# Recurrent attention and a gated feed-forward on one core: diagonal sums of five groups by wide TensorE products, and a new order of loads and steps

## The chip, the cores and the metric

One Trainium2 chip, one of its cores. The metric is the device time of one execution in microseconds. The core has five engines that run their own queues of instructions in order: TensorE (PE in the rows, its weight loads PEld), VectorE (DVE), ScalarE (ACT), GpSimd (POOL) and SyncE (SP, which here only issues DMAs). They wait for one another by semaphores.

## The reference

Four sequences of 768 steps with 8 heads of 48: a state of 48 x 48 per head decays by w, takes the outer product of k and v, and is read by r; the current step is weighted by u. The result goes through a feed-forward with a convolution over three steps and a sigmoid gate.

```
for t in range(S):
    kt, vt, rt = (k[:, :, t], v[:, :, t], r[:, :, t])
    cur = np.einsum('bhd,bhe->bhde', u[None] * kt, vt)
    y[:, :, t] = np.einsum('bhd,bhde->bhe', rt, state + cur)
    state = w[None, :, :, None] * state + np.einsum('bhd,bhe->bhde', kt, vt)
# x = y as (B, S, 384)
h = np.maximum(x @ w_in, 0.0)
conv_out = sum(conv_w[k] * hp[:, k:k + S, :] for k in range(3))   # hp: h padded
gate = 1.0 / (1.0 + np.exp(-conv_out))
return h * gate @ w_out
```

## The kernel before

**Attention.** The 4 x 768 steps are cut into 24 groups of 128 steps (GT), each of two chunks of 64 (C). Heads lie in pairs, one on partitions 0 to 47, the other on 64 to 111, so that two products run on separate halves of the array. A group has k and r feature-major (tile KR; its halves are called KK and RR), k, r and v token-major (TOK, three slots) and a score tile SC; four buffers each of KR and TOK turn round (NBUF), two of SC. `prep(g)` scales KR by powers of the decay, makes the scaled token-major k, and writes the diagonal of SC: for each step and head the sum over features of u k r, on the diagonal by a multiplication with `eye`. `visit(g, av, su)` is the work of PE: for group g the outputs AV (from state and from scores), and for group g+1 the scores SP and the state sums UP. After it VectorE copies SP into SC under a mask (line 659) and forms the two new states SS, each M + UP, where M is the old state times the decay. Visit -1 does group 0's scores only; visit 2 is split in two halves.

**How the diagonal sum is made before.** Groups 0 and 1 (NE = 2): VectorE multiplies KK by RR into SC, sixteen TensorE products of one column each (line 573) sum over features against `uw`, and VectorE multiplies by `eye` from PSUM (line 582). From group 2 on: GpSimd multiplies token-major r by k (KRT) and by u (KRU), VectorE sums (line 592), GpSimd multiplies by `eye`. Token-major k is made from KR by PE for group 0 alone (NK = 1, line 565, with a copy by ScalarE, line 576); later groups load it and GpSimd multiplies it by the tile TH (KS). TH itself comes from PE (line 491) and a ScalarE copy.

**Feed-forward.** Seven units of columns, each in eight slices. `first` is the product with w_in (line 741, into the banks HP0 and HP1), then ScalarE's relu and scale (749, 750), two convolution steps on VectorE (753), the sigmoid (756), the gate (757). `second` is the product with w_out (788 for the first unit, in full precision; 791 for the others, in three rounded products, for which the result is split in a high and a low part). The weights are loaded as w_in and w_out pieces of 384 KB into three staging buffers ST, converted on ScalarE and VectorE (504, 507, 509: the tile WF) and split into two rounded parts (ScalarE line 515; GpSimd the low part). The first unit reads the attention's output from XF; rows of head 6 and 7 are moved there by small DMAs from SBUF to SBUF, by SP and ScalarE.

**Order.** All steps are written down as a plan (`op`) with their reads and writes. `Plan.late` gives each step a due time, `MOVES` shifts due times, and `Plan.order` picks for each engine the next step; the engines then run these lists in order. Where PE would be without work before the first `second`, filler products of a zero tile `wz` (line 874) are put. Group loads and weight loads (classes in LONG) are limited: one may be issued only when the sixth before it has landed (LOADS = 6), from the fortieth on the fourth before it. Line 382 issues all DMAs, line 373 all `tensor_tensor` steps.

Of the kernel before, what the change touches and what calls it, by code (L numbers as in the profile page):

```python
# [16 lines left out]
C = 64  # L17
# [22 lines left out]
LONG, LOADS = ('ldK', 'ldT', 'ldV', 'wdma'), 6  # L40
NE = 2
NK = 1
# [19 lines left out]
FBASE, FETCH, FIRST, LATER = 3.4, 0.7, 40, 4  # L62
GATED = 4
DIRECT, ACTQ = (2,), (1,)
# [28 lines left out]
class Plan:  # L93
# [36 lines left out]
    def late(self):  # L130
# [16 lines left out]
        for seed, share, sigma, near in self.moves:  # L147
            x = seed
            for i in range(n):
                x = (x * 1103515245 + 12345) & 0x7fffffff  # L150
                u = x / 2147483648.0
                x = (x * 1103515245 + 12345) & 0x7fffffff
                if u < share and (not near or abs(late[i] - near) < 15.0):
                    late[i] += sigma * (2.0 * (x / 2147483648.0) - 1.0)
        return late

    def order(self):
# [25 lines left out]
        def fetched(s, t, k):  # L183
# [5 lines left out]
            while count > len(there) - 0.4:  # L189
                at_ = max(s, s + (len(there) - 0.4 - a) * d, there[-1])  # L190
                there.append(at_ + FBASE + FETCH * sum(1 for z in large[-8:] if z > at_))
# [5 lines left out]
        while todo:  # L197
            best = None
            for e in self.ENG:
# [13 lines left out]
                if e in ("sp", "act"):  # L213
                    y = large[-LOADS] if LOADS <= len(large) < FIRST else large[-LATER] if len(large) >= FIRST else 0.0
                    for i in av:
                        if self.dma[i]:
                            ready[i] = max(ready[i], lanes[0], y if ops[i][4] in LONG else 0.0)
# [52 lines left out]
            elif self.dma[i]:  # L270
# [5 lines left out]
                if cls in LONG:  # L276
                    large.append(done)
# [25 lines left out]
def rwkv_ffn_kernel(tc, krd, krt, vt, wd, ut, w_in, conv_w, w_out, out):  # L303
# [4 lines left out]
    with ExitStack() as ctx:  # L308
# [71 lines left out]
        def dma(rd, wr, dst, src, dur=0.5, x=0.1, cls="", q="sp", gate=None):  # L380
            def issue(e):
# [3 lines left out]
                if cls in LONG:  # L385
                    k = LOADS if len(loads) < FIRST else LATER
                    if len(loads) >= k:
                        tc.add_manual_dep(i.ins, loads[-k].ins.name, behind_, reason="loads")
                    loads.append(i)
# [146 lines left out]
        def bank(g):  # L536
            return [(HP[0], ("HP", 0)), (HP[1], ("HP", 1)), (PO[1], ("PO", 1))][g] if g < 3 else (UP, "UPq")

        def prep(g):
# [14 lines left out]
            if g < NE:  # L554
                kb, key = bank(g)
                pp = s[0:112].rearrange("q p c t -> q p (c t)")
                tt("dve" if g < 3 else ANY, 512, kr(i), [("SC", g % 2)], "P", out=pp, in0=KK[i][0:112], in1=RR[i][0:112], op=ALU.mult)

                def mm(e):
                    for c in range(2):  # L560
                        for p in range(NP):
                            for x in range(2):
                                r = slice(64 * x, 64 * x + D)
                                n = (p * 2 + c) * D
                                PE.matmul(kb[64 * x:64 * x + C, n:n + D], KK[i][r, p, c * C:(c + 1) * C], D64[r, p], start=True, stop=True)

                def mq(e):
                    for c in range(2):
                        for p in range(NP):
                            for x in range(2):  # L570
                                r = slice(64 * x, 64 * x + D)
                                n = NP * 2 * D + p * 2 + c
                                PE.matmul(kb[64 * x:64 * x + C, n:n + 1], s[r, p, c], uw[r, p:p + 1], start=True, stop=True)
                if g < NK:
                    op("pe", 1.1, [k for k in kr(i) if k[0] == "KK"] + ["D64"], [key], mm, "pks", 1700, mode=1, k=32)
                    op("act", act(384), [key], [("tK", i)], lambda e: A.copy(k_t.rearrange("q p c d -> q (p c d)"), kb[:, 0:NP * 2 * D]), "KSc")
                else:
                    tt(ANY, 384, ["TH"], [("tK", i)], "KS", out=k_t, in0=k_t, in1=TH.unsqueeze(2).broadcast_to([128, NP, 2, D]), op=ALU.mult)
                op("pe", 1.1, [("SC", g % 2), "uw"], [key], mq, "pq", 1200, mode=1, k=32)
                q = kb[:, NP * 2 * D:NP * 2 * D + H]  # L580
                if g < 3:
                    op("dve", dve(512, psum=1), [key, "eye"], [("SC", g % 2)], lambda e: V.tensor_tensor(
                        out=s.rearrange("q p c t -> q (p c) t"), in0=eye.unsqueeze(1).broadcast_to([128, 2 * NP, C]), in1=q.unsqueeze(2).broadcast_to([128, 2 * NP, C]), op=ALU.mult), "dg")
                    return
                op("act", 0.2, [key], [("QQ", g % 2)], lambda e: A.copy(QQ[g % 2], q), "qc")
                diagonal(g)
# [351 lines left out]
```

## Time and profile before

| what | value |
|---|---|
| median of 3 timed runs | 301.81 us (300.54 to 302.5) |
| profiled execution: span, first to last instruction | 302.5 us |
| PE busy | 287.7 us, 95% of the span |
| VectorE, ScalarE, GpSimd busy | 222.5, 176.4, 166.2 us |
| bytes moved by DMA | 37.00 MB, mean 122 GB/s |

The page's first part has each engine's busy time. The windows view gives it for stretches between two times, with the clock that PE was granted (1.00 is full speed). In the timeline a row is one or several instructions in a row of one kind: start, duration, engine, line, what is written and read, count, and in brackets the idle time ahead with what ended it. TensorE works an f32 product in two recorded passes, so that a product of the order counts as two records in the trace.

### The profile page before, as it was taken

To read this page: it belongs to the slowest core of one execution; us is meant where nothing else is said; L and a number is where in the kernel's file an instruction comes from. 1 tells how busy PE (TensorE), PEld (TensorE's weight loads), DVE (VectorE), ACT (ScalarE), POOL (GpSimd) and SP (SyncE) were. 2 spreads that over 40 slices of the span, in tenths; PEclk is the share of its full clock that TensorE was granted. 3 is DMA by queue.
4 is the path that set the end of the run, shared out by engine and by line. 5 is a ranking of instruction groups with operands and counts; after the bars stand their busy time and mean duration, and the time that the engine had idled before them with its cause. 6 is when DMAs were issued, how large, how long until landed. Compare 5 with 4: busy or idle time off the path is not lost.

```text
span 302.5 us, 9831 instructions
## 1 busy us (share of the span) xinstructions
PE 287.7 (95%) x4104; PEld 239.2 (79%) x4110; DVE 222.5 (74%) x359; ACT 176.4 (58%) x348; POOL 166.2 (55%) x196
## 2 busy tenths in 40 slices
PE   7979999869998999999999999999999999999994
PEld 2657666546777888889888888888888988899993
DVE  5766579896998876877879984899867755556561
ACT  3135484857776456664656753667735665556663
POOL 8367686984678884787735846658511111131230
PEclk9997999998999999999999999999999999999999
DMA  6994695855655535646424453554210020001102
GB/s 155 226 240 130 201 278 158 243 166 158 187 176 154 148 106 146 178 119 172 141 75 126 114 179 64 133 139 143 75 49 14 15 96 7 9 0 62 33 0 78
DMA packets 24011, 37.00 MB, mean 122 GB/s; under 512 B 6256, under 2 KB 16784, under 8 KB 23968
## 3 DMA queue, kind: packets, MB, share of 16 engines
q1 hardware_dynamic: 23632, 36.04, 42.7%
q8 instruction: 32, 0.52, 0.7%
q10 hardware_dynamic: 336, 0.35, 0.5%
q14 instruction: 11, 0.09, 0.1%
HBM read 29.49 MB, written 4.72 MB: 113 GB/s over the span
## 4 chain that ended last, share of the span: by engine, by line
PE 67%; DMA 6%; DVE 5%; POOL 4%; issue 3%; SPq 2%; ACT 2%; POOLq 0%; DVEq 0%; ACTq 0%
PE HP L741 29%; PE PO L791 25%; PE SP L638 4%; POOL TOK L373 3%; PE AV L654 3%; PE PO L788 3%; DMA TOK<-in_krt_dram 2%; PE AV L647 2%; SPq L382 2%; PE UP L651 2%; DMA KR<-in_krd_dram 1%; DMA ST<-in_w_in_dram 1%; DVE CV L753 1%; DVE KR L373 1%; DMA XF<-XF 1%
## 5 line engine op out<-in xcount | busy, mean ns | idle before, releaser
L741 PE MATMUL HP<-XT,wi 128*128 128x464 f32 (+2 forms) x432 | 98.8, 373 | 0.2 <-DVE CV L757 0.2
L791 PE MATMUL PO<-GG,wo 128*128 128x462 f32 (+2 forms) x432 | 97.5, 369 | 0.7 <-POOL GG L763 0.7
L753 DVE SCALAR_TENSOR_TENSOR CV<-HP,cw,CV 128x462 f32<-128x462 f32 (+2 forms) x112 | 75.2, 672 | 21.2 <-ACT CV L750 19.9
L791 PEld LDWEIGHTS PO<-GG,wo 128*128 128x128 f32 x432 | 80.2, 189 | 9.7 <-POOL GG L763 0.9
L741 PEld LDWEIGHTS HP<-XT,wi 128*128 128x128 f32 x432 | 79.5, 189 | 9.6 <-issue 0.4
L763 POOL TENSOR_TENSOR GG<-CV,GG 128x462 fp32r<-128x462 f32 (+2 forms) x30 | 34.7, 1156 | 65.6 <-ACT GG L762 61.0
L749 ACT ACTIVATE HP<-HP 128x464 f32<-128x464 f32 (+2 forms) x56 | 29.3, 523 | 50.4 <-PE HP L741 50.3
L638 PE MATMUL SP<-KR 48*64 48x64 f32 x768 | 46.3, 233 | 5.6 <-DVE KR L373 4.1
L757 DVE TENSOR_TENSOR CV<-HP,CV 128x462 f32<-128x462 f32 (+2 forms) x56 | 34.3, 612 | 21.3 <-ACT CV L756 21.0
L638 PEld LDWEIGHTS SP<-KR 48*64 48x64 f32 x768 | 38.9, 137 | 12.2 <-DVE KR L373 5.9
L654 PE MATMUL AV<-SC,TOK 64*48 64x64 f32 x760 | 47.0, 223 | 0.0
L647 PE MATMUL AV<-KR,SS 48*48 48x64 f32 x696 | 43.8, 223 | 0.0
L756 ACT ACTIVATE CV<-CV 128x462 f32<-128x462 f32 (+2 forms) x56 | 31.9, 569 | 19.8 <-DVE CV L753 19.6
L651 PE MATMUL UP<-TOK 64*48 64x48 f32 x704 | 41.3, 209 | 2.2 <-DVE SS L373 2.2
L750 ACT ACTIVATE CV<-HP,cw 128x462 f32<-128x462 f32 (+2 forms) x56 | 35.1, 627 | 2.3 <-ACT HP L749 0.4
L651 PEld LDWEIGHTS UP<-TOK 64*48 64x48 f32 x704 | 34.1, 127 | 2.3 <-DVE SS L373 2.3
L654 PEld LDWEIGHTS AV<-SC,TOK 64*48 64x48 f32 x760 | 35.7, 124 | 0.0
L647 PEld LDWEIGHTS AV<-KR,SS 48*48 48x48 f32 x696 | 32.5, 123 | 2.0 <-issue 2.0
L373 POOL TENSOR_TENSOR SC<-eye,QQ 128x512 f32<-128x512 f32 x22 | 23.4, 1064 | 18.0 <-PE AV L654 14.2
L762 ACT CAST GG<-CV 128x462 fp32r<-128x462 f32 (+2 forms) x48 | 27.2, 566 | 9.5 <-DVE CV L757 9.1
L373 POOL TENSOR_TENSOR TOK<-TOK 128x384 f32<-128x384 f32 x22 | 22.6, 1027 | 17.9 <-DMA TOK<-in_krt_dram 17.9
L373 POOL TENSOR_TENSOR MM<-SS,w 112x192 f32<-112x192 f32 x36 | 19.0, 528 | 17.1 <-DVE SS L373 15.7
(85 smaller groups left out, 358.8 us busy)
## 6 DMA issues: line engine op xcount, KB each, us to landing
KR<-in_krd_dram SPq DMA_DIRECT2D x46, 192.0 KB, 4.1
TOK<-in_krt_dram SPq DMA_DIRECT2D x22, 384.0 KB, 4.4
TOK<-in_vt_dram SPq DMA_DIRECT2D x47, 96.0 KB, 3.5
ST<-in_w_in_dram SPq DMA_DIRECT2D x8, 384.0 KB, 3.8
ST<-in_w_out_dram SPq DMA_DIRECT2D x8, 384.0 KB, 3.8
XT<-XT SPq DMA_DIRECT2D x126, 16.0 KB, 2.0
out_dram<-OS SPq DMA_DIRECT2D x6, 193.0 KB, 2.0
out_dram<-OS SPq DMA_DIRECT2D x5, 191.0 KB, 2.2
```

Of the source, the lines that this page charges most:

```text
L373: op(eng, d, rd, wr, lambda e: e.tensor_tensor(**kw), cls, port=not psum)
L638: PE.matmul(SP_[xs[x], p, c], KK[j][rows[x], p, t], RR[j][rows[x], p, t], start=True, stop=True)
L647: PE.matmul(outs[x], state(2 * g + c)[rows[x], p], RR[i][rows[x], p, t], start=not direct, stop=False)
L651: PE.matmul(UP[rows[x], n:n + D], TOK[j][xs[x], 0, p, c], TOK[j][xs[x], 2, p, c], start=True, stop=True)
L654: PE.matmul(outs[x], TOK[i][xs[x], 2, p, c], SC[g % 2][xs[x], p, c], start=none and not direct, stop=True)
L741: PE.matmul(hp[:, at:at + n_], WF[f][:, 0, j * 128:j * 128 + 128] if full else wi[a][:, j, fs], XF[:, j, c0:c0 + w] if full else src(x, j, y),
L750: op("act", act(n, 0, 1), [H_, "cw"], [("T", ti)], lambda e: A.activation(t1, hp[:, 1:n + 1], AF.Copy, scale=cw[:, 3 * f + 1:3 * f + 2]), ...
L753: op("dve", dve(n, psum=1) + 0.02, [H_, "cw"], [("T", ti)], lambda e, k=k: V.scalar_tensor_tensor(out=t1, in0=hp[:, k:n + k], scalar=cw[:, ...
L756: op("act", act(n, 1), [], [("T", ti)], lambda e: A.activation(t1, t1, AF.Sigmoid), "SG")
L757: op("dve", dve(n), [H_], [("T", ti)], lambda e: V.tensor_tensor(out=t1, in0=hp[:, 1:n + 1], in1=t1, op=ALU.mult), "GG")
L763: op("any", {"dve": dve(n), "pool": pool(n, "GL")}, [("T", ti), ("GH", gi)], [("GL", gi)], lambda e: e.tensor_tensor(out=gg(gi)[:, 1, :n], ...
L791: PE.matmul(po[:, :n], wo[a][:, f, ms], gg(gi)[:, x, :n], start=f == 0 and j == 0, stop=f == NF - 1 and j == 2)
```

## The change

- **Groups 0 to 4 get their diagonal sum from PE** (NE = 5). The operands change places: the weights are `uw`, repeated over 64 columns, and SC runs through as 128 columns: eight products of 128 columns a group in place of sixteen of one column. Each row of the result holds the sums, and the `eye` step (VectorE, from PSUM) keeps the diagonal. For groups 2 to 4 this replaces KRT, KRU, the reduce and GpSimd's `eye` step, and token-major r isn't loaded (192 KB each). The result of groups 3 and 4 goes into the bank SP, which visits use too. For groups 2 to 4 the planner may give the product of KK and RR to GpSimd.
- **Token-major k of groups 0 and 1 by PE** (NK = 2): one more set of line 565, one ScalarE copy; 192 KB fewer loaded, and no KS for group 1.
- **Limit on loads under way by size**: 6.0 units (384 KB are 1.28 to 1.3) for the first 36, then 4.2, in place of six, later four loads.
- **The planner** reckons code fetches of PE by the load queue, `MOVES` may also shift a run of steps by a fixed time, and its table is another. So all engines' orders change, fillers too: 62 before and 38 now.

```diff
-LONG, LOADS = ('ldK', 'ldT', 'ldV', 'wdma'), 6
-NE = 2
-NK = 1
+LONG, WAY = ('ldK', 'ldT', 'ldV', 'wdma'), 6.0
+FIRST, LATER = 36, 4.2
+NE = 5
+NK = 2
...
-FBASE, FETCH, FIRST, LATER = 3.4, 0.7, 40, 4
+FBASE, FETCH = 3.4, 0.8
...
-    (982228, 0.4, 3.0, 105.0), (679522, 0.004, 3.0, 75.0), (769013, 0.03, 1.0, 105.0), (831907, 0.03, 3.0, 45.0),
+    (384, 32.0, -1.23, -1.0), (160731, 0.1, 3.0, 120.0), (601551, 0.4, 8.0, 30.0), (630, 4.0, 0.36, -1.0),
...
+            if near < 0:
+                for i in range(seed, min(n, seed + int(share))):
+                    late[i] += sigma
+                continue
...
-                    k = LOADS if len(loads) < FIRST else LATER
-                    if len(loads) >= k:
-                        tc.add_manual_dep(i.ins, loads[-k].ins.name, behind_, reason="loads")
-                    loads.append(i)
+                    k, way = len(loads), x
+                    lim_ = WAY if k < FIRST else LATER
+                    while k and way <= lim_:
+                        k -= 1
+                        way += loads[k][1]
+                    if way > lim_:
+                        tc.add_manual_dep(i.ins, loads[k][0].ins.name, behind_, reason="loads")
+                    loads.append((i, x))
...
-            return [(HP[0], ("HP", 0)), (HP[1], ("HP", 1)), (PO[1], ("PO", 1))][g] if g < 3 else (UP, "UPq")
+            return [(HP[0], ("HP", 0)), (HP[1], ("HP", 1)), (PO[1], ("PO", 1))][g] if g < 3 else (SP_.rearrange("q p c t -> q (p c t)"), "SUs")
...
+                ks, kkey = (PO[1], ("PO", 1)) if g < 2 else (HP[0], ("HP", 0))
...
-                tt("dve" if g < 3 else ANY, 512, kr(i), [("SC", g % 2)], "P", out=pp, in0=KK[i][0:112], in1=RR[i][0:112], op=ALU.mult)
+                tt("dve" if g < 2 else "any", 512, kr(i), [("SC", g % 2)], "P", out=pp, in0=KK[i][0:112], in1=RR[i][0:112], op=ALU.mult)
...
                 def mq(e):
-                    for c in range(2):
-                        for p in range(NP):
-                            for x in range(2):
-                                r = slice(64 * x, 64 * x + D)
-                                n = NP * 2 * D + p * 2 + c
-                                PE.matmul(kb[64 * x:64 * x + C, n:n + 1], s[r, p, c], uw[r, p:p + 1], start=True, stop=True)
+                    for p in range(NP):
+                        for x in range(2):
+                            r = slice(64 * x, 64 * x + D)
+                            PE.matmul(kb[64 * x:64 * x + C, p * GT:(p + 1) * GT], uw[r, p:p + 1].broadcast_to([D, C]), s[r, p].rearrange("q c t -> q (c t)"), start=True, stop=True)
...
-                if g < 3:
-                    op("dve", dve(512, psum=1), [key, "eye"], [("SC", g % 2)], lambda e: V.tensor_tensor(
-                        out=s.rearrange("q p c t -> q (p c) t"), in0=eye.unsqueeze(1).broadcast_to([128, 2 * NP, C]), in1=q.unsqueeze(2).broadcast_to([128, 2 * NP, C]), op=ALU.mult), "dg")
-                    return
-                op("act", 0.2, [key], [("QQ", g % 2)], lambda e: A.copy(QQ[g % 2], q), "qc")
-                diagonal(g)
+                op("pe", 0.95, [("SC", g % 2), "uw"], [key], mq, "pq", 2100, mode=1, k=16)
+                op("dve", dve(512, psum=1), [key, "eye"], [("SC", g % 2)], lambda e: V.tensor_tensor(
+                    out=s.rearrange("q p c t -> q (p c) t"), in0=eye.unsqueeze(1).broadcast_to([128, 2 * NP, C]), in1=kb.rearrange("q (n t) -> q n t", t=C), op=ALU.mult), "dg")
```

The order at three places (61 to 64 in the names KR, TOK are the four buffers, so groups 0 to 3 at first; 69 and 70 those of SC). SP's issues from the program's start, before:

```order
L382 DMA wc<-in_wd_dram 48x4
L382 DMA uc<-in_ut_dram 48x4x1
L382 DMA KR_61<-in_krd_dram 64x1024
L382 DMA TOK_65<-in_vt_dram 64x384
L382 DMA TOK_66<-in_krt_dram 128x384
L382 DMA uc<-in_ut_dram 48x4x1
L382 DMA KR_62<-in_krd_dram 48x1024
L382 DMA uu<-in_ut_dram 128x192
L382 DMA KR_62<-in_krd_dram 48x1024
L382 DMA TOK_66<-in_vt_dram 64x384
L382 DMA TOK_67<-in_krt_dram 128x768
L382 DMA KR_63<-in_krd_dram 48x1024
```

and now:

```order
L405 DMA KR_61<-in_krd_dram 64x1024
L405 DMA uc<-in_ut_dram 48x4x1
L405 DMA wc<-in_wd_dram 48x4
L405 DMA KR_62<-in_krd_dram 48x1024
L405 DMA TOK_65<-in_vt_dram 64x384
L405 DMA KR_62<-in_krd_dram 48x1024
L405 DMA uc<-in_ut_dram 48x4x1
L405 DMA TOK_66<-in_vt_dram 64x384 x2
L405 DMA KR_63<-in_krd_dram 48x1024 x2
L405 DMA TOK_67<-in_krt_dram 128x384
L405 DMA TOK_67<-in_vt_dram 64x384 x2
L405 DMA ST_100<-in_w_in_dram 128x768
```

Group 0's KR stands ahead of `wc`, both halves of KR of groups 1 and 2 stand earlier, and group 1's token-major k is gone. In both, ScalarE issues the rest of `wc`, the other half of group 0's KR (192 KB) and of its v (96 KB) at the same time.

VectorE between the `eye` step of group 1 and the state sums that visit 1 waits for, before:

```order
L582 TENSOR_TENSOR SC_70<-eye,HP_126 128x512
L509 SCALAR_TENSOR_TENSOR WF_89<-ST_100 128x384
L373 TENSOR_TENSOR SS_74<-MM_75,UP 112x192
L659 COPY_PREDICATED SC_70<-mask,SP 128x512
L373 TENSOR_TENSOR KR_64<-KR_64,PO_129 112x1024
L373 TENSOR_TENSOR SS_71<-MM_76,UP 112x192
```

and now:

```order
L606 TENSOR_TENSOR SC_70<-eye,HP_126 128x512
L536 SCALAR_TENSOR_TENSOR WF_89<-ST_100 128x384
L680 COPY_PREDICATED SC_70<-mask,SP 128x512
L396 TENSOR_TENSOR SS_74<-MM_75,UP 112x192
L536 SCALAR_TENSOR_TENSOR ST_99<-ST_99 128x24
L396 TENSOR_TENSOR wi_118<-WF_89,wi_117 128x3x128
L396 TENSOR_TENSOR KR_64<-KR_64,PO_129 112x1024
L396 TENSOR_TENSOR SS_71<-MM_76,UP 112x192
```

The last state sum SS_71 stands behind the scaling of group 3 (KR_64) in both; a weight split (wi_118), which GpSimd did, has come in ahead of it.

PE at the first line 741 (762 now) and group 4, now:

```order
L762 MATMUL HP_125<-XF,WF_89 128x384 x3
L762 MATMUL HP_126<-XF,WF_90 128x384 x3
L599 MATMUL SP<-SC_69,uw 64x128 x8
L659 MATMUL SP<-KR_61 64x64 x2
L668 MATMUL AV<-KR_64,SS_73 48x64 x2
L672 MATMUL UP<-TOK_65 48x48 x2
```

Group 4's diagonal sum into SP stands between the first two slices of the feed-forward and visit 3, whose first product writes SP as well; before, visit 3 came directly behind the six products.

## Rows read from the trace of the kernel before

**Rows 1.** The page, part 1: busy us, share of the span, instructions

```profile
PE 287.7 (95%) x4104; PEld 239.2 (79%) x4110; DVE 222.5 (74%) x359; ACT 176.4 (58%) x348; POOL 166.2 (55%) x196
```

**Rows 2.** Windows: length, busy us (x records) by engine, granted clock, DMA, GB/s

```profile
16.10:18.10 2.00, 1.97 (x118) 1.95 (x118) 2.00 (x4) 1.13 (x3) 0.61 (x1) 1.00 1.04 259
18.10:23.20 5.10, 2.80 (x19) 1.18 (x19) 3.36 (x7) 1.84 (x6) 3.50 (x4) 0.99 0.79 206
23.20:26.70 3.50, 3.45 (x120) 3.33 (x122) 1.87 (x3) 2.14 (x6) 2.43 (x3) 0.52 0.33 107
28.40:33.10 4.70, 4.59 (x161) 4.53 (x162) 1.38 (x3) 2.20 (x6) 2.32 (x4) 1.00 0.65 205
41.50:66.30 24.80, 20.24 (x290) 12.71 (x289) 22.85 (x34) 17.51 (x39) 20.45 (x21) 1.00 0.71 213
66.30:71.90 5.60, 5.59 (x119) 4.18 (x120) 4.71 (x8) 2.40 (x6) 3.65 (x4) 0.70 0.51 143
71.90:94.10 22.20, 20.72 (x307) 15.20 (x306) 19.11 (x30) 16.19 (x33) 14.77 (x16) 1.00 0.61 175
94.10:302.50 208.40, 204.21 (x2620) 181.92 (x2619) 149.18 (x238) 123.83 (x232) 99.18 (x107) 1.00 0.32 90
```

**Rows 3.** Timeline of PE up to the first product with w_in

```profile
7.35 1.13 PE L565 MATMUL HP<-D,KR 48*64 48x48 f32 x32 [0.32 <-POOL D L478]
...
9.17 1.09 PE L573 MATMUL HP<-uw,SC 48*64 48x1 f32 x32
10.13 0.31 PE L638 MATMUL SP<-KR 48*64 48x64 f32 x4
...
10.36 0.30 PE L638 MATMUL SP<-KR 48*64 48x64 f32 x4
...
12.22 1.03 PE L874 MATMUL PO<-wz 128*128 128x512 bf16 x4 [0.16 <-issue]
13.18 0.67 PE L491 MATMUL SP<-ident,DN 48*64 48x48 f32 x16
...
18.23 2.54 PE L874 MATMUL PO<-wz 128*128 128x512 bf16 x11 [0.16 <-issue]
...
23.23 0.32 PE L651 MATMUL UP<-TOK 64*48 64x48 f32 x2 [2.21 <-DVE SS L373]
...
35.52 4.04 PE L741 MATMUL HP<-XF,WF 128*128 128x384 f32 x12
```

**Rows 4.** Timeline of VectorE

```profile
7.50 0.17 DVE L480 TENSOR_TENSOR uw<-uc,PW 112x4 f32<-112x4 f32 x1 [0.72 <-DMA uc<-in_ut_dram]
...
10.19 0.69 DVE L373 TENSOR_TENSOR KR<-KR,PO 112x512 f32<-112x512 f32 x1 [1.21 <-DMA KR<-in_krd_dram]
10.80 0.68 DVE L582 TENSOR_TENSOR SC<-eye,HP 128x512 f32<-128x512 f32 x1
...
15.87 1.28 DVE L373 TENSOR_TENSOR KR<-KR,PO 112x512 f32<-112x512 f32 x2 [1.20 <-DMA KR<-in_krd_dram]
...
21.69 1.22 DVE L373 TENSOR_TENSOR KR<-KR,PO 112x1024 f32<-112x1024 f32 x1 [1.08 <-DMA KR<-in_krd_dram]
22.83 0.35 DVE L373 TENSOR_TENSOR SS<-MM,UP 112x192 f32<-112x192 f32 x1
...
62.19 2.67 DVE L509 SCALAR_TENSOR_TENSOR WF<-ST 128x384 int32<-128x384 int32 x1
```

**Rows 5.** Timeline of GpSimd: the `eye` step of group 2

```profile
18.25 1.04 POOL L373 TENSOR_TENSOR SC<-eye,QQ 128x512 f32<-128x512 f32 x1 [1.54 <-DVE SC L582]
```

**Rows 6.** DMA view up to 35.5 us: queue; issues with median us to landing

```profile
q8 instruction: 5, 0.08, 1.0%
...
KR<-in_krd_dram SPq DMA_DIRECT2D x8, 192.0 KB, 5.2
...
XF<-XF ACTq DMA_DIRECT2D x3, 16.0 KB, 3.9
```

**Rows 7.** Waits of PE over the whole span: total us, times, longest

```profile
PE SP L638 <- issue: 1.5, 1, 1.5
```

More of the change, by code (lines that the diff above doesn't have):

```diff
@@ L61 @@
 FN, FE, FW = 512, 6000, 3.4
-FBASE, FETCH, FIRST, LATER = 3.4, 0.7, 40, 4
+FBASE, FETCH = 3.4, 0.8
 GATED = 4
+DIRECT, ACTQ = (2,), (1,)
 DIRECT, ACTQ = (2,), (1,)
@@ L190, in fetched @@
                 at_ = max(s, s + (len(there) - 0.4 - a) * d, there[-1])
-                there.append(at_ + FBASE + FETCH * sum(1 for z in large[-8:] if z > at_))
+                there.append(at_ + FBASE + 1.1 * FETCH * max(0.0, dq - at_ - 0.9))
             for b in range(1, len(there)):
@@ L213, in order @@
                 if e in ("sp", "act"):
-                    y = large[-LOADS] if LOADS <= len(large) < FIRST else large[-LATER] if len(large) >= FIRST else 0.0
                     for i in av:
                         if self.dma[i]:
-                            ready[i] = max(ready[i], lanes[0], y if ops[i][4] in LONG else 0.0)
+                            ready[i] = max(ready[i], lanes[0])
+                            if ops[i][4] in LONG:
+                                k, way = len(large), ops[i][1]
+                                lim_ = WAY if k < FIRST else LATER
+                                while k and way <= lim_:
+                                    k -= 1
+                                    way += large[k][1]
+                                if way > lim_:
+                                    ready[i] = max(ready[i], large[k][0])
                 lim = min(max(f, ready[i]) for i in av) + DELTA
@@ L276, in order @@
                 if cls in LONG:
-                    large.append(done)
+                    large.append((done, x))
             else:
@@ L385, in issue @@
                 if cls in LONG:
-                    k = LOADS if len(loads) < FIRST else LATER
-                    if len(loads) >= k:
-                        tc.add_manual_dep(i.ins, loads[-k].ins.name, behind_, reason="loads")
-                    loads.append(i)
+                    k, way = len(loads), x
+                    lim_ = WAY if k < FIRST else LATER
+                    while k and way <= lim_:
+                        k -= 1
+                        way += loads[k][1]
+                    if way > lim_:
+                        tc.add_manual_dep(i.ins, loads[k][0].ins.name, behind_, reason="loads")
+                    loads.append((i, x))
             op(q, dur, rd, wr, issue, cls, x, dma=True, gate=gate)
@@ L564, in mm @@
                                 n = (p * 2 + c) * D
-                                PE.matmul(kb[64 * x:64 * x + C, n:n + D], KK[i][r, p, c * C:(c + 1) * C], D64[r, p], start=True, stop=True)
+                                PE.matmul(ks[64 * x:64 * x + C, n:n + D], KK[i][r, p, c * C:(c + 1) * C], D64[r, p], start=True, stop=True)
                 def mq(e):
-                    for c in range(2):
-                        for p in range(NP):
-                            for x in range(2):
-                                r = slice(64 * x, 64 * x + D)
-                                n = NP * 2 * D + p * 2 + c
-                                PE.matmul(kb[64 * x:64 * x + C, n:n + 1], s[r, p, c], uw[r, p:p + 1], start=True, stop=True)
+                    for p in range(NP):
+                        for x in range(2):
+                            r = slice(64 * x, 64 * x + D)
+                            PE.matmul(kb[64 * x:64 * x + C, p * GT:(p + 1) * GT], uw[r, p:p + 1].broadcast_to([D, C]), s[r, p].rearrange("q c t -> q (c t)"), start=True, stop=True)
@@ L574, in prep @@
                 if g < NK:
-                    op("pe", 1.1, [k for k in kr(i) if k[0] == "KK"] + ["D64"], [key], mm, "pks", 1700, mode=1, k=32)
-                    op("act", act(384), [key], [("tK", i)], lambda e: A.copy(k_t.rearrange("q p c d -> q (p c d)"), kb[:, 0:NP * 2 * D]), "KSc")
+                    op("pe", 1.1, [k for k in kr(i) if k[0] == "KK"] + ["D64"], [kkey], mm, "pks", 1700, mode=1, k=32)
+                    op("act", act(384), [kkey], [("tK", i)], lambda e: A.copy(k_t.rearrange("q p c d -> q (p c d)"), ks[:, 0:NP * 2 * D]), "KSc")
@@ L577, in prep @@
                 else:
                     tt(ANY, 384, ["TH"], [("tK", i)], "KS", out=k_t, in0=k_t, in1=TH.unsqueeze(2).broadcast_to([128, NP, 2, D]), op=ALU.mult)
-                op("pe", 1.1, [("SC", g % 2), "uw"], [key], mq, "pq", 1200, mode=1, k=32)
-                q = kb[:, NP * 2 * D:NP * 2 * D + H]
-                if g < 3:
-                    op("dve", dve(512, psum=1), [key, "eye"], [("SC", g % 2)], lambda e: V.tensor_tensor(
-                        out=s.rearrange("q p c t -> q (p c) t"), in0=eye.unsqueeze(1).broadcast_to([128, 2 * NP, C]), in1=q.unsqueeze(2).broadcast_to([128, 2 * NP, C]), op=ALU.mult), "dg")
-                    return
```

50 rows, old and new, of the table MOVES are left out of this document.

## The prediction

> **What bounds the kernel now.** I read the page's busy shares first: TensorE (PE) is busy for 95% of the span [rows 1], so the span is PE's own work plus the places where PE does nothing, does filler, or runs slowly. The windows table finds them [rows 2]. From 94.1 us to the end PE is busy for 204.2 of 208.4 us; nothing of size can be won there unless PE's work itself changes. Ahead of 94.1 there are three idle places: 2.3 us in the window from 18.1 (2.80 of 5.10 busy), 4.6 us from 41.5 (20.24 of 24.80) and 1.5 us from 71.9 (20.72 of 22.20). Two stretches have a low granted clock: 0.52 from 23.2, where 120 records of a visit took 3.45 us against 118 records in 1.97 us at 16.1 (1.5 us lost), and 0.70 from 66.3 (0.30 x 5.6 = 1.7 us lost). And until the first feed-forward product (line 741) at 35.52 us PE is kept busy with filler products of `wz`: eleven took 2.54 us [rows 3], 0.23 us each.
>
> So the start, up to 35.5 us, is set by something else. PE's 2.21 us wait at 23.23 [rows 3] ended with a state sum SS on VectorE; that sum ran at 22.83, right behind the scaling of group 3's k and r, which had waited for its load until 21.69 [rows 4]. The scalings of groups 1 and 2 waited for their loads too (10.19 and 15.87). The loads of k and r set the start.
>
> **Loads.** Each such wait dates a landing. By the order of SP's and ScalarE's issues, 1312 KB stand up to group 1's second KR load, 2368 KB up to group 2's, 3640 KB up to group 3's; between 10.19 and 21.69 us that is 2328 KB in 11.5 us, 202 KB/us. The changed order has 1024, 1600 and 3256 KB up to the same loads, because token-major k of group 1 and token-major r of groups 2 to 4 (192 KB each) aren't loaded and `uu` and the small loads stand later. At 202 KB/us group 1's scaling can start at 10.19 - 1.4 = 8.8 us, group 2's at 8.8 + 2.9 = 11.7, group 3's at 11.7 + 8.2 = 19.9. A larger limit on loads under way keeps the queue full; I give it no gain of its own, since each load already took 5.2 us to land [rows 6], which is queueing. The other end is a loss: a small transfer that is issued behind a fuller queue lands later, and rival 4 prices that for code.
>
> SP now issues group 0's 256 KB ahead of `wc` and `uc`. At 202 KB/us that delays the decay powers by up to 1.3 us, by nothing if the queue is free; I take 1.0, as the queue is loaded from the first microsecond. VectorE waited 0.72 us for `uc` between the two scalings of group 0 [rows 4], and that step now stands behind them, so I cost the pair at 0.3 us, hidden before the first visit at 10.1, whose group 0 work otherwise stays.
>
> **PE's own order up to the first line 741.** The order holds 62 fillers before and 38 after, one of the difference lying later: 23 x 0.23 = 5.3 us less. Token-major k of group 1 by PE costs what group 0's cost, 1.1 us [rows 3]. The new diagonal sum is eight products of 128 columns instead of sixteen of one column. Its price isn't in the trace. The nearest row is the visit, where two pairs on separate halves of the array, of 64 and 48 columns, come every 0.23 us (10.13 to 10.36). So 128 columns cost 0.26 us a pair, 1.0 us for four pairs; with no overlap of the halves 2.0; at the 1.1/16 us of a token-major product 0.55. I take 1.0, as operands lie on the same two halves, which equals the old 1.09 us. Two more groups (2, 3) before the first line 741 add 2.0. After the first visit, which ends at 12.1 (the filler row 0.16 us behind it), stand k and sum of group 1 (2.1), visit 0 (2.0), line 491 (0.7), group 2's sum (1.0) and twelve fillers (2.8) [rows 3], to 20.7; the state sum stands behind group 3's scaling as before (1.22 and 0.35 us), now at 19.9 + 1.6 = 21.5. With that short wait the low clock should not return: 1.5 less. The idle goes from 2.3 to 0.8. Sum: -5.3 + 1.1 + 2.0 - 1.5 - 1.5 = -5.2, line 741 at 30.3.
>
> The other engines allow a little less. From visit 1 at 21.5 the chain is that visit 2.0, five fillers 1.1, the split visit's two halves 4.6 (the window from 28.4, [rows 2]), and between them group 3's sum 1.0 and six fillers 1.4, which cover the `eye` step: 31.6. The moves of XF take 3.9 us from issue to landing [rows 6]; ScalarE now issues the last of them behind its copy of the split visit's first half, near 27, so they too end near 31. I take 31.2, inside the two sums, a gain of **4.3 us**. Ends: 30.3 if the loads are never late, 35.5 if they land as before.
>
> **Behind it.** Group 4's sum stands between line 741 and visit 3, with no filler around it. It costs 1.0 us, and as it now writes the bank SP, the visit's first product waits for VectorE to read it: 0.68 us for the `eye` step on PSUM (line 582, [rows 4]) and about 0.5 us of the two convolution steps queued ahead. **+2.2 us.** Queued behind that wait are all of visit 3 and its products; no cover.
>
> GpSimd loses two products on token-major k and r and the `eye` step of three groups, and one step of group 1: ten steps of about 1.04 us [rows 5]; it gains three products k x r of 512 elements at 1.04: 7 us less. VectorE gains three `eye` steps, loses three reduces that are a little shorter, and takes two of the weight splits from GpSimd: about 1.5 us more. ScalarE gains one copy and loses the small ones. None ends a wait alone. They act through the 4.6 + 1.5 + 1.7 = 7.8 us lost between 41.5 and 94.1: of these waits one stands behind a weight step on VectorE that took 2.67 us at 62.19, against 0.68 us for a step on a third more elements (line 582, [rows 4]); GpSimd is at work beside it, so I hold a lighter GpSimd for a help. The rest is order, which changes throughout. Ends: all 7.8 goes, or all stays. I let a third go, **-2.5 us**, since loads and GpSimd are lighter but VectorE is not.
>
> **Sum.** 302.5 - 4.3 + 2.2 - 2.5 = 297.9 us against the profiled span of 302.5. That span is 0.7 us above the median 301.81 of the timed runs, so **297.2 us**.
>
> **The rivals.** (1) *No stall returns.* The four waits between 41.5 and 94.1 disappear with the lighter queue: 5.3 us less, 292 us. For it: my chain meets no engine that is late by then. Against: VectorE is already busy 22.85 of 24.8 us from 41.5 [rows 2].
>
> (2) *VectorE paces the middle.* In the same window it has 1.95 us to spare, and gets 1.5 us more; PE starts earlier and waits there instead. The 2.5 is not won and 1 to 2 us of the start is returned: 299.7 + 1.5 = 301 us.
>
> (3) *The clock.* Twenty-four fillers fewer may leave PE quiet around the visits. The row from 23.2 shows 0.52, the 1.2 GHz level, right after 2.3 us of idling, and a visit cost 1.5 us more there. If three visits and the first six line 741 products run so, 3 x 1.5 + 1.7 = 6.2 us: 303.4. Against: new products fill 4 us of the place of the fillers. The Trainium skill, "TensorE: Matmul & The Clock Gate", section "What's actually happening", makes the throttled state the default that activity lifts; the trace agrees, with 0.52 after the wait and 1.00 around the fillers. By that rule alone this change would come out at 303.4.
>
> (4) *Slower: code for PE.* Its instructions come by DMA (queue q8, five blocks up to 35.5 us, [rows 6]), and the waits table has 1.5 us in one piece in which no engine released PE [rows 7]. If a block queued like a load, half as much again under way would make 5.2 us into 7.8, 2.6 us more a block; three such blocks on the path give 7.8 us: 305 us. From 7.6 us above my forecast, or some 1.5 us for each of the five blocks, it decides. Against: PE has waited for no engine's signal only once so long. The Trainium skill, "Runtime: NRT & Kernel Launch", section "Instruction fetch mechanics", says each sequencer fetches the next page through its own queue while it runs the current one, mostly hidden. By that rule this rival costs nothing; the 1.5 us in the waits table is against "mostly hidden", if it was code, which this trace doesn't tell.
>
> **How the numbers follow.** Forecast 0.45 (294 to 298.8), stall-free 0.12, VectorE pacing 0.20, clock 0.10, code 0.13. A measurement of this kernel tells about 1%, 3 us, from no change: faster means under 298.8, slower over 304.8. The first two and 0.06 of the third are faster: 0.63. The rest of the third, 0.14, and the clock's, 0.10, are no change: 0.24. The code case is slower: 0.13. The range reaches from 293.0 (half of the stall-free cases lie below, 0.06) to 304.0 (the code cases lie above, 0.13), leaving out under 2 in 10. The forecast's own range is 294 to 298.8.
>
> **What would show it.** Right: the first diagonal sums at about 1.0 us each; visit 0 near 14 us, visit 1 from 21.5 without the 0.52 clock; line 741 at 31 us and visit 3 near 37; PE idle between 41.5 and 94.1 of some 4 us. Wrong: group 3's scaling still near 21.7 (then loads are not served earlier), `wc` landing beyond 5 us, a granted clock near 0.5 in the first 40 us, waits without a releaser before 35 us, or VectorE full with PE waiting in the middle.

## The result: slower, 305.3 us for 301.5

| what | before | after |
|---|---|---|
| median of the timed runs on one chip | 301.47 us (300.54 to 302.5) | 305.33 us (304.51 to 305.42) |
| ratio, 95% interval | | 1.0121 (1.0082 to 1.016) |
| profiled execution: span | 302.5 us | 303.5 us |

The forecast was 297.2 us, the range 293 to 304: wrong in direction and in size. Below, "before" and "after" are the two kernels. A timed figure stands 1.7 us above the span of the same execution (305.24 for 303.5). The execution of before that was profiled was a slow one (304.27 us, 2.8 above the median), as was the one profiled in section 3 of the experiments (304.26, 3.0 above its median). So a second profile of before was taken later, with a span of 299.3 (301.0 timed); "typical before" below is that one.

The page of the profile after, part 1 (as [rows 1]):

```profile
PE 288.2 (95%) x4131; PEld 240.9 (79%) x4134; DVE 222.4 (73%) x362; ACT 177.0 (58%) x349; POOL 158.5 (52%) x186
```

GpSimd lost 7.7 us of work (7 forecast), VectorE is as busy as before (1.5 more forecast). What went wrong is in the windows of after (columns as in [rows 2]):

```profile
6.58:9.56 2.98, 0.00 (x0) 0.03 (x1) 2.51 (x8) 1.15 (x4) 1.00 (x7) 0.96 1.09 198
9.56:18.63 9.07, 9.06 (x163) 8.14 (x165) 5.45 (x11) 1.45 (x4) 0.57 (x2) 0.64 0.60 162
...
92.60:98.53 5.93, 4.18 (x13) 3.67 (x14) 3.49 (x5) 3.00 (x6) 4.64 (x5) 0.71 0.62 194
98.53:303.50 204.97, 201.08 (x2596) 179.05 (x2594) 145.96 (x235) 121.57 (x228) 96.39 (x103) 1.00 0.30 85
```

PE stands still for 3.0 us from 6.58 and then has a mean granted clock of 0.64 for 9 us; there is a second hole of 1.75 us at 92.6, again with a slow clock behind it. From 98.53 on PE is busy 201.1 of 205.0 us; in typical before it is 201.1 of 205.6 (from 93.75), so nothing is lost there.

VectorE, then PE, in the timeline of after:

```profile
6.30 0.57 DVE L491 TENSOR_TENSOR_SCAN PW<-wc,wz 112x32 f32<-112x32 f32 x4 [3.84 <-DMA wc<-in_wd_dram]
...
8.78 1.28 DVE L396 TENSOR_TENSOR KR<-KR,PO 112x512 f32<-112x512 f32 x2
```

```profile
9.56 1.94 PE L593 MATMUL PO<-D,KR 48*64 48x48 f32 x32 [2.99 <-issue]
11.44 1.04 PE L895 MATMUL PO<-wz 128*128 128x512 bf16 x2
12.41 1.97 PE L599 MATMUL HP<-SC,uw 48*64 48x128 f32 x16
...
16.80 1.10 PE L593 MATMUL PO<-D,KR 48*64 48x48 f32 x32
17.74 1.05 PE L599 MATMUL HP<-SC,uw 48*64 48x128 f32 x16
...
36.32 4.14 PE L762 MATMUL HP<-XF,WF 128*128 128x384 f32 x12
40.39 1.09 PE L599 MATMUL SP<-SC,uw 48*64 48x128 f32 x16
42.34 0.27 PE L659 MATMUL SP<-KR 48*64 48x64 f32 x2 [0.86 <-DVE SC L606]
```

The scan that needs `wc` runs at 6.30, where it ran at 3.39 in the profile before. SP issued its piece of that load at 2.07, behind 256 KB of KR; before it issued it at 0.80. The DMA view up to 8 us, before and then after (KB, us from issue to landing):

```profile
wc<-in_wd_dram SPq DMA_DIRECT2D x1, 0.8 KB, 1.6
```

```profile
KR<-in_krd_dram SPq DMA_DIRECT2D x1, 256.0 KB, 3.6
...
wc<-in_wd_dram SPq DMA_DIRECT2D x1, 0.8 KB, 4.1
```

So the piece landed at about 6.2 us in place of 2.4: 1.3 us because it was issued later, and 2.5 because it was longer under way. (Before, the scan waited last for a piece of `wc` that ScalarE had issued, so it came 2.9 us later and not 3.8.) The scaling of KR follows at 8.78, and the first product with KR at 9.56. The same pair of steps (`pks`, the products that make token-major k, line 593, and the diagonal sum, line 599) takes 1.94 and 1.97 us there and 1.10 and 1.05 us at 16.80: nearly twice as long, the lower of the two clock levels. The wait of 2.99 is put down to "issue", but the experiments below tie it to `wc`.

Where PE stands, in us from the span's start:

| | before, first profile | typical before | after | after with wc first |
|---|---|---|---|---|
| first line 741 (762) | 35.52 | 34.95 | 36.32 | 32.06 |
| visit 3 | 39.49 | 38.91 | 42.34 | 38.09 |
| end of visit 8 | 94.49 | 91.09 | 92.60 | 88.50 |
| first product with w_in behind it | 95.22 | 91.82 | 95.43 | 90.20 |
| span | 302.5 | 299.3 | 303.5 | 297.9 |

Against typical before, after is 1.4 late at line 762, 3.4 at visit 3, 1.5 at the end of visit 8, then 3.6, and 4.2 at the end.

### The profile page after: what moved, and what is told of

Its sections match the earlier page's. It is cut to its first block, busy times and chain, and to the rows that moved or that the text cites. A ratio compares the mean times of both kernels' runs of the same rounds, so it can differ in the third digit from the quotient of the medians.

```text
span 303.5 us, 9879 instructions
## 1 busy us (share of the span) xinstructions
PE 288.2 (95%) x4131; PEld 240.9 (79%) x4134; DVE 222.4 (73%) x362; ACT 177.0 (58%) x349; POOL 158.5 (52%) x186
## 4 chain that ended last, share of the span: by engine, by line
PE 73%; DMA 8%; DVE 5%; issue 4%; ACT 3%; SPq 3%; POOL 2%; DVEq 0%; ACTq 0%; POOLq 0%
PE HP L762 29%; PE PO L812 26%; PE SP L659 5%; PE AV L675 3%; DMA out_dram<-OS 3%; SPq L405 3%; PE AV L668 2%; PE UP L672 2%; DMA TOK<-in_vt_dram 2%; PE PO L895 2%; DMA TOK<-in_krt_dram 1%; DMA wc<-in_wd_dram 1%; DVE CV L774 1%; DVE WF L536 1%; PE PO L809 1%
## 5 line engine op out<-in xcount | busy, mean ns | idle before, releaser
L774 DVE SCALAR_TENSOR_TENSOR CV<-HP,cw,CV 128x462 f32<-128x462 f32 (+2 forms) x112 | 75.2, 671 | 20.9 <-ACT CV L771 19.9
L762 PEld LDWEIGHTS HP<-XT,wi 128*128 128x128 f32 x432 | 80.6, 191 | 9.8 <-DVE WF L536 0.6
L659 PE MATMUL SP<-KR 48*64 48x64 f32 x768 | 45.3, 230 | 0.9 <-DVE SC L606 0.9
L675 PE MATMUL AV<-SC,TOK 64*48 64x64 f32 x760 | 45.1, 217 | 0.0
L668 PE MATMUL AV<-KR,SS 48*48 48x64 f32 x696 | 42.1, 217 | 0.0
L672 PE MATMUL UP<-TOK 64*48 64x48 f32 x704 | 40.4, 206 | 0.2 <-DMA TOK<-in_vt_dram 0.2
L675 PEld LDWEIGHTS AV<-SC,TOK 64*48 64x48 f32 x760 | 34.6, 119 | 0.0
L396 POOL TENSOR_TENSOR MM<-SS,w 112x192 f32<-112x192 f32 x35 | 19.8, 565 | 23.1 <-DVE SS L396 13.6
L668 PEld LDWEIGHTS AV<-KR,SS 48*48 48x48 f32 x696 | 31.5, 119 | 0.3 <-DVE CV L778 0.3
L396 POOL TENSOR_TENSOR TOK<-TOK 128x384 f32<-128x384 f32 x19 | 19.5, 1028 | 16.7 <-DMA TOK<-in_krt_dram 16.7
L396 POOL TENSOR_TENSOR SC<-eye,QQ 128x512 f32<-128x512 f32 x19 | 20.1, 1055 | 13.4 <-PE AV L675 9.3
```

The source lines that it names most:

```text
L396: op(eng, d, rd, wr, lambda e: e.tensor_tensor(**kw), cls, port=not psum)
L659: PE.matmul(SP_[xs[x], p, c], KK[j][rows[x], p, t], RR[j][rows[x], p, t], start=True, stop=True)
L668: PE.matmul(outs[x], state(2 * g + c)[rows[x], p], RR[i][rows[x], p, t], start=not direct, stop=False)
L672: PE.matmul(UP[rows[x], n:n + D], TOK[j][xs[x], 0, p, c], TOK[j][xs[x], 2, p, c], start=True, stop=True)
L675: PE.matmul(outs[x], TOK[i][xs[x], 2, p, c], SC[g % 2][xs[x], p, c], start=none and not direct, stop=True)
L762: PE.matmul(hp[:, at:at + n_], WF[f][:, 0, j * 128:j * 128 + 128] if full else wi[a][:, j, fs], XF[:, j, c0:c0 + w] if full else src(x, j, y),
```

## The experiments

Ratios are to the kernel before on the same chip, with 95% intervals. The medians of before there were 301.5, 301.4 and 302.0 us in the three groups of runs.

**1. The late wc, undone and done alone.** In the changed kernel, SP's list:

```diff
+wc <- in_wd
 KR_61 <- in_krd 64x1024
 uc <- in_ut
-wc <- in_wd
```

> The changed kernel with one load moved: SyncE issues its piece of wc first again, ahead of the 256 KB K rows and of uc. Theory A (the late wc costs the start): wc lands by about 4 and not at 6.2, VectorE has the diagonals some 2.3 earlier, TensorE's 3.0 of idle time ahead of the first pks shrinks below 1, pks and pq run at the full clock (about 0.95 and 0.9 for 1.88 and 1.76), visit 0 starts about 4 earlier than 18.6, and the time falls from about 305 to 301, if the start binds the end. Rival (the start is not what binds: later waits take the gain back): visit 0 is earlier all the same, but the time stays within 1.5 of 305.

And in the kernel before, the opposite:

```diff
-wc <- in_wd
 uc <- in_ut
 KR_61 <- in_krd 64x1024
+wc <- in_wd
```

> The kernel before with one load moved: SyncE issues its piece of wc right behind its first 256 KB K rows, as the changed kernel does. Theory A: wc lands some 2 later, VectorE's diagonals and TensorE's first work start as much later, TensorE idles long enough to drop to half clock, and the time rises by about 3 (to 304.5). Rival (TensorE has slack there before the 5.3 stall that ends at 35.5, which swallows it): less than 1.

Measured: with wc first 299.71 us, ratio 0.994 (0.9903 to 0.9978), 5.6 us less than the change as it came and faster than before. Before with wc late: 306.66 us, 1.0163 (1.0101 to 1.0225). The theory holds from both sides, and the price was larger than expected both times. Timeline of VectorE, then PE, with wc first:

```profile
2.91 0.57 DVE L491 TENSOR_TENSOR_SCAN PW<-wc,wz 112x32 f32<-112x32 f32 x4 [0.46 <-DMA wc<-in_wd_dram]
```

```profile
7.40 1.14 PE L593 MATMUL PO<-D,KR 48*64 48x48 f32 x32 [0.29 <-POOL D L505]
...
9.67 1.09 PE L599 MATMUL HP<-SC,uw 48*64 48x128 f32 x16 [0.60 <-DVE uw L507]
```

The scan runs 3.4 us earlier, and PE's wait "for issue" is 0.3. So it was the data and not PE's code. Windows of the kernel before with wc late:

```profile
6.29:9.87 3.58, 0.00 (x1) 0.03 (x1) 2.93 (x10) 1.19 (x4) 2.00 (x8) 1.00 1.10 207
9.87:17.06 7.19, 6.83 (x130) 6.28 (x133) 3.21 (x6) 0.48 (x1) 1.99 (x2) 0.61 0.87 195
```

The same hole and a low clock behind it, in a kernel without any of the other edits; its first line 741 came at 39.76, 4.8 later than in typical before. Here the first products behind the hole still ran at full speed (1.13 us), and the sum behind them was slow (1.87).

**2. The wait or the clock?** Thirteen more fillers ahead of the first `pks`, the loads untouched:

```diff
+filler x13   (line 895)
 pks of group 0   (line 593)
```

> The changed kernel, its loads as they are, with 13 more filler products of wz ahead of the first pks, where TensorE idled 3.0 and came back at half clock. It separates the two parts of theory A: the fillers cover the wait without ending it, so pks begins about 9.6 as before, but at the full clock: pks 1.07 for 1.88, pq 0.9 for 1.76, visit -1 1.9 for 2.64. If the clock is a part of the loss, visit 0 starts 2.4 earlier than 18.6 and the time falls by about 2 to 303. Rival (the diagonals, not TensorE, set the pace up to visit 0, so the slow clock costs nothing there): visit 0 within 0.5 of 18.6, time within 1 of 305.

Measured: 0.9994 (0.9968 to 1.002), 301.47 us: 3.8 us less than after, with `wc` as late as in after (the scan runs at 6.56). Windows:

```profile
1.38:9.52 8.14, 8.14 (x26) 3.06 (x26) 3.46 (x10) 2.64 (x6) 5.64 (x18) 1.00 0.95 181
9.83:15.92 6.09, 5.93 (x162) 5.61 (x164) 5.45 (x11) 1.45 (x4) 0.57 (x2) 1.00 0.82 233
```

PE computes nothing more of use, starts `pks` at 9.83 for 9.56, and reaches visit 0 at 15.92 for 18.63 at the full clock; line 762 starts at 33.63 for 36.32. So of the 4.3 us between after and wc first at line 762, 2.7 are the clock behind the hole. The other 1.6 are what the earlier data still gave; with wc first PE was also held by the stop that the next section describes.

**3. The second piece of uc.** With wc first, VectorE waited 1.29 us for the other half of `uc`, and PE 0.6.

```diff
 KR_61 <- in_krd 64x1024
 uc <- in_ut
+uc <- in_ut
 KR_62 <- in_krd 48x1024
 ...
-uc <- in_ut
```

> The kernel with wc first again, and besides the second piece of uc issued right behind the first, ahead of group 1's rows. There VectorE waited 1.29 for that piece (it landed 5.2 after its issue) and TensorE 0.6. Theory (any small load behind large ones on that queue lands 4 to 5 later, and what needs it waits): uw is made about 1 earlier, TensorE's 0.6 goes, the time falls by 0.5 to 1 from 299.7. Rival (group 1's rows, now behind it, or the 1.36 in visit 0 that no engine ended, set that place): within 0.4 of 299.7.

Measured: 0.9957 (0.9923 to 0.999), no different from wc first. The sum of group 0 indeed started at 9.02 for 9.67, but the gain was gone in visit 0. PE's timeline with wc first, then with uc too:

```profile
16.55 0.21 PE L675 MATMUL AV<-SC,TOK 64*48 64x64 f32 x1 [1.36 <-issue]
```

```profile
16.53 0.21 PE L675 MATMUL AV<-SC,TOK 64*48 64x64 f32 x1 [2.00 <-issue]
```

PE stopped behind the 46th record of visit 0 in both, at 15.19 and at 14.53, and went on at 16.55 and 16.53. In the kernel of experiment 4 it stopped at the same record, from 14.58 to 16.67, and in the second profile of wc first from 15.96 to 16.98. In that of experiment 2, with 13 products more ahead, it stopped behind the 33rd record, 13 earlier, and went on at 17.29. The place is fixed by the count of PE's instructions and not by data, and the DMA view shows one block of the instruction queue q8 (0.52 MB in 32 blocks, so 16 KB each) under way ahead of it:

```profile
q8 instruction: 1, 0.02, 5.5%
```

(q8 between 13.9 and 15.2 us, wc first.) In windows of 0.1 us that block stands at 13.7 (with uc too), 13.9 (wc first), 14.0 (experiment 4), 14.2 (wc first, second profile) and 14.7 (experiment 2); PE went on 2.6 to 2.8 us behind it each time. I take it for the code that PE waits for; no run changed the code itself. In after the block came at 15.3, and PE was at visit 0 only at 18.63: no such wait.

**4. The price at visit 3, and the stores.** On top of the last kernel:

```diff
 f1 slice 0   (line 762, PE)
+diagonal sum of group 4 -> SP
 f1 slice 1
-diagonal sum of group 4 -> SP
@@ VectorE: its eye step ahead of two convolution steps
@@ SP
+out <- OS_97
 TOK_68 <- in_krt
+out <- OS_98
 TOK_68, KR_63, KR_64, TOK_67
-out <- OS_97, OS_98
```

> The last kernel with two more moves. Group 4's diagonal sum stands between the two first slices and its eye step ahead of two convolution steps on VectorE (there visit 3 waited 0.86 for it): this price goes, less some 0.3 of waiting for GpSimd's product of k and r, so 0.5. The first two stores of the output are issued ahead of three to four group loads (there TensorE waited 0.96 for the store's landing): a store issued 1.5 earlier lands 1.5 earlier, if landing is the bytes under way over the rate, and the 0.96 goes. Together 1.5 less than the kernel before it in this call, about 297.5. Rival (the loads that are put behind come late instead, and visits wait for them): no gain, or a loss of 1.

Measured: 1.0013 (0.9984 to 1.0043). The forecast gain of 1.5 us did not come; the ratio is about 1.7 us above that of the kernel it was built on, but the two intervals overlap. The copy no longer waited for the store (PE still waited 0.7 us for the copy), but group 4's sum then waited 0.73 us for GpSimd's product of k and r, and a later slice 1.7 us for a convolution step, 1.2 before the move. The stores alone, with wc first, beside wc first once more:

> The kernel with wc first, and of the later two moves only the stores: the first two are issued ahead of three or four group loads, uc and group 4's sum stay where the change has them. Theory (the stores' landing is the wait near 90; the code that TensorE waited for inside visit 0 made earlier work there worthless, so uc is left alone): TensorE's wait for the output copy (0.96 in the profile with wc first) goes, 0.5 to 1 less than the kernel with wc first in this call, about 299. Rival (the loads put behind are needed at once): the same time or more.

> The changed kernel with wc first, the same as in the first of these runs, on the chip of this call: to set it beside the kernel that also has the stores ahead. If the first measurement holds, about 0.994 of before, 299.7.

Measured: 0.996 (0.9933 to 0.9987) and 0.9954 (0.9924 to 0.9984). The two can't be told apart. So wc first is the version to keep: faster than both kernels, by 0.5 to 0.6% than before, in two sets of runs.

**5. The hole at 92.6.** ScalarE's copies of the output in after; the third goes into the buffer of the first:

```profile
86.50 0.87 ACT L822 ACTIVATE OS<-PO 128x382 f32<-128x382 f32 x2
...
93.81 0.49 ACT L822 ACTIVATE OS<-PO 128x382 f32<-128x382 f32 x1 [3.18 <-DMA out_dram<-OS]
```

The store of the first was issued at 88.52 and took 5.2 us to land, as the loads around it did; the DMA view of after from 78 to 90 us (KB each, median us to landing):

```profile
KR<-in_krd_dram SPq DMA_DIRECT2D x6, 192.0 KB, 5.9
...
out_dram<-OS SPq DMA_DIRECT2D x1, 191.0 KB, 5.2
```

In the kernel before, its first store landed 2.2 us after issue (3.0 in typical before). First try: the three first stores by ScalarE, on its own queue.

```diff
-SP:  out <- OS (first three)
+ACT: out <- OS (each right behind its copy)
```

> The changed kernel with its first three stores issued by ScalarE, each right behind the copy that it stores, in place of SyncE's queue among the loads. Theory B (the first store queues behind some ten loads on its queue, landed 5.2 after its issue where it took 2.2 before, and the next copy into its buffer and with it TensorE wait at 92.6): the first store lands within 3 of its issue, the copy does not wait for it, TensorE's 1.75 idle and the 0.72 clock after it go, and the time falls by about 3.2 to 302. Rival (the DMA engines themselves are full from 80.9 to 92.6, whatever the queue; or the wait only moves): 1 or less.

Measured: 1.0126 (1.0055 to 1.0196), as after. The first store took 5.7 us to land from that queue as well. So the queue is not what delays it; the DMA engines' share in 78 to 90 us was 0.94 (0.92 in after). (The Trainium skill, "DMA: Bandwidth & Descriptors", section "Issuing engines are not separate DMA queues", says that all issuers share the same 16 engines; this trace agrees, 5.7 us for 5.2.) The wait only moved: the copy waited 0.72 us for the store and PE 0.70 for the copy, but PE now waited 1.73 us for a state sum at 92.97. Nor does a full share alone set the landing: with the first two stores ahead of the loads (section 4) the share was 0.92 too, and their median 3.2 us. Second try: the limit by count in the changed kernel.

```diff
-lim_ = WAY if k < FIRST else LATER   (bytes)
+k = 6 if len(loads) < 40 else 4      (loads)
```

> The changed kernel with the rule of before for loads under way: a count (6, from the 40th on 4) and not bytes. Theory C (the byte limit lets more loads run at once in the middle, so each lands later, 5.2 to 6.6 after issue for 2 to 4 before, and the first store with them): landings of the loads issued from 78 to 88 return to 3 or 4, the stall at 92.6 goes, the time falls by about 3. At the start 6 loads hold less than 1.8 MB, so some loads may come later and take up to 1 back there. Rival (the limit is not what delays them, the order is): less than 0.5 either way.

Measured: 1.0372 (1.0322 to 1.0421), 313.04 us. From 85 us on the loads landed 3 to 4 us after issue again, but SP, which issues in order, was held at each load, and the store behind them went out at 94.12 for 88.52. SP's timeline, then PE's waits (total us, times, longest):

```profile
91.32 2.24 SPq L405 DMA_DIRECT2D KR<-in_krd_dram  x2
93.61 0.47 SPq L405 DMA_DIRECT2D TOK<-in_vt_dram  x1
94.12 0.58 SPq L405 DMA_DIRECT2D out_dram<-OS  x1
```

```profile
PE PO L808 <- ACT OS L818: 5.2, 2, 3.6
```

PE's waits for the output copies grew from 1.8 to 5.2 us; the rest of the 7.7 us is not traced. So my theory had the sign wrong: in this order the larger limit is a help. And alone, in the order of before:

```diff
-k = LOADS if len(loads) < FIRST else LATER   (loads)
+lim_ = 6.0 if k < 36 else 4.2                (bytes)
```

> The kernel before in its own order, with the changed kernel's limit by bytes (6.0 units, then 4.2) in place of six and four loads. It measures the limit alone. Theory (more bytes under way make each load land later, and SyncE is held up less; which of the two wins depends on the order that was made for the limit): landings in the middle rise from 2 to 4 toward 5 or 6, and the time moves by less than 1.5 either way. Rival (the larger limit is a gain or a loss of its own): more than 1.5 from 301.5.

Measured: 1.0028 (1.0003 to 1.0052), under 1 us: no gain of its own. Nor did the landings rise toward 5 or 6 as expected: 4.0 to 4.8 us from 78 to 92, for 3.7 to 4.6 before. So the larger limit alone does not make the landings of after. What the hole costs in the timed runs stays open: with wc first it was 0.96 us in one profile and 2.07 in the other, both at the full clock; with the stores ahead the copy no longer waited for a store, and the median did not move.

**6. Before once more.**

> The kernel before once more, unchanged, for a second profile: the first had a span of 302.5, and the time of its run was 304.3, which is 2.5 above the median of 301.8. If the 1.5 wait without a releaser at 92.6, the 2.66 wait at 63.6 and the 0.70 clock behind it were of that one execution, this profile shows them smaller, with the first product with w_in again at 35.5 and a span near 300. If they belong to the kernel, they stand again, and the span outside the median must come from elsewhere.

Measured: 301.78 us, 1.0028 (0.999 to 1.0065); span 299.3. Windows:

```profile
23.30:25.22 1.92, 1.92 (x120) 1.84 (x122) 0.80 (x2) 1.92 (x6) 1.89 (x3) 1.00 0.04 10
...
67.23:71.19 3.96, 3.96 (x19) 2.38 (x13) 2.99 (x6) 3.63 (x8) 1.98 (x2) 1.00 0.71 189
```

The visit that took 3.45 us at a clock of 0.52 in [rows 2] takes 1.92 here, and the stretch that had 0.70 has 1.00. The 1.5 us wait of [rows 7] is 0.68. The 2.66 wait ahead of visit 6 stands again, with 2.68. So these losses in [rows 2] and [rows 7] were of that one execution; the two spans differ by 3.2 us.

## Why the prediction was wrong, step by step

- **The failed step: "that delays the decay powers by up to 1.3 us ... I take 1.0 ... I cost the pair at 0.3 us, hidden before the first visit at 10.1".** The powers came 2.9 us later, and nothing hid it: the first visit began at 14.17, and line 762 at 36.32 for the forecast 31.2. The bound of 1.3 was 256 KB at the average rate. SP's two issues ahead of `wc` alone took 1.3 us, which the sum did not count; and `wc` then took 4.1 us to land for 1.6, 1.8 us behind the landing of the 256 KB issued ahead of it (0.81 + 3.6 = 4.4). So a place in a byte count does not date a small load; what held it up is not shown. The sum also left out what an idle PE turns into: the hole of 3.0 us brought the half clock for `pks`, sum and visit. Priced by the runs: 5.0 to 5.6 us in all (the two measurements of wc first), of which 3.8 go when the hole is filled with useless products, with the data no earlier. I had named "`wc` landing beyond 5 us" as a sign of being wrong; it was that, at about 6.2; the low clock in the first 40 us that I had named came too (0.64 from 9.56 to 18.63).
- **Fewer fillers.** They were counted as 5.3 us saved. Up to the first `pks` two of them less (13 for 15) and the wait 2.9 us longer left PE bare. The clock rival ended at 303.4, near the measured time by luck: the low clock came in another stretch and from another cause, the hole and not a thin mix of work.
- **Loads: earlier, as forecast, and no longer the bound.** The one landing that dates the forecast is group 1's, in the kernel with wc and uc first: its scaling waited for KR until 9.31 (8.8 forecast). With wc first the scalings of groups 2 and 3 wait for no load. That of group 3 ran at the forecast 19.9 by luck, behind a weight split on VectorE:

```profile
19.24 0.74 DVE L396 TENSOR_TENSOR wi<-WF,wi 128x384 fp32r<-128x384 f32 x1
19.90 1.22 DVE L396 TENSOR_TENSOR KR<-KR,PO 112x1024 f32<-112x1024 f32 x1
```

- **PE's prices: right.** In the rows at the full clock the sums take 1.05 to 1.09 us (1.0 forecast), `pks` 1.10 to 1.14 (1.1), and visit 3 is delayed by 1.09 + 0.86 = 1.95 us (2.2).
- **Line 741 at 31.2:** 32.06 with wc first. On the way PE waited 0.60 us for `uc` and 1.36 in the stop of visit 0; how the 0.9 is shared between them is not shown. If the stop is code, rival 4 had a real mechanism, once and not three times, but it is no part of the slowdown: after had no such stop. That rival 4's 305 us is the measured time is luck.
- **The base.** Span (302.5) and median (301.81) were taken as one scale; like for like the profiled execution was 2.5 above that median. The -1.5 for the slow clock, and the share of the 7.8 us that I let go for the 1.5 and 1.7 in [rows 2, 7], were gains against one execution and not against the median. That is why the version with wc first, whose span of 297.9 equals the forecast's sum to the digit, is only 1.4 to 1.8 us faster in the timed runs. The equality is luck: against the first profile it gained 3.5 us up to line 741 (4.3 forecast), lost 2.1 to visit 3 (2.2) and gained 3.2 behind it (2.5).
- **Behind line 741:** between visit 3 and the end of visit 8 after won 1.9 us on typical before (4.7 on the first profile, which the 2.5 forecast was counted on), then lost 2.1 at the hole at 92.6. VectorE as the pacer (rival 2) shows, beside the 0.86 ahead of visit 3, in two waits only, 1.3 and 1.1 us (the 1.8 is the hole):

```profile
PE PO L812 <- ACT OS L822: 1.8, 1, 1.8
...
PE HP L762 <- DVE CV L778: 1.3, 1, 1.3
PE PO L809 <- DVE WF L536: 1.1, 1, 1.1
```

The 1.3 stands behind a weight step on VectorE of 3.45 us at 63.62; a lighter GpSimd did not shorten it (2.67 in [rows 4]); GpSimd was at work beside it until 66.66.

## What to carry to other kernels

When a reordered load list gains bandwidth, look first at the smallest load on the longest chain, and count the issues ahead of it as well as the bytes: 768 bytes moved behind 256 KB cost 5 to 5.6 us here, more than all the rest of the change brought. Price a hole on TensorE as the hole plus the half-clock work behind it, and keep filler there until the data can come. How much slow work follows has to be read from a trace each time: with the stores ahead, a wait of 0.89 us was followed by 4.2 us at a clock of 0.60, and in the second profile with wc first waits of 1.37 and 1.17 us by work at 1.00. Take two profiles of the kernel before, and compare spans with spans, before counting its stalls as gains.

## What the runs showed that was not expected

- In after the loads of 96 to 384 KB and the store that were issued between 78 and 90 us landed 5.2 to 5.9 us later (medians) with the DMA engines at 0.92, and a store from ScalarE's queue took 5.7. A limit that brings the loads to 3 to 4 us cost 7.7 us in that order, where SP stood still at each load and the stores behind went out 5.6 us later.
- A stop of PE at a fixed place in its instruction stream ended 2.6 to 2.8 us behind one block of the instruction queue, however early PE came: at 16.5 to 16.7 us where it came at 14.53, 14.58 or 15.19, after 2.00, 2.09 and 1.36 us. An earlier start was worth nothing beyond it.
